# Gelu in one ScalarE activation in a fused attention and GEGLU kernel

## The chip, the cores and the metric

The kernel runs on one core of a Trainium2 chip. A core has five engines with a queue each: TensorE (PE, matrix products, with its weight loads shown apart as PEld), VectorE (DVE), ScalarE (ACT, activation functions), GpSimd (POOL) and SyncE (SP, which here only issues DMAs). The metric is the time of one execution on the device in microseconds; three runs of the kernel before were timed.

## The reference

A layer norm, then two branches of the same normalised rows, whose results are multiplied. `S` is 2048, `D` 576, `H` 32 heads of 18, `F` 4608, all in float32.

```python
xn = layernorm(x)
q, k, v = split(xn @ wqkv)                        # 32 heads of 18
s = concat(softmax(q @ k.T * 18 ** -0.5) @ v) @ wo
ff = (gelu(xn @ w_gate, approximate=True) * (xn @ w_up)) @ w_down
out = x + s * silu(ff)
```

The tanh form of Gelu is `0.5 * z * (1 + tanh(0.7978845608 * (z + 0.044715 * z ** 3)))`.

## The kernel before, in words

After a prologue (layer norm, transposes, the projections to q, k and v) the kernel is a row of 144 sections, `FF["n"]` counting them. A section computes the gate sums `pg` and the up sums `pu` of one block of 128 of the 4608 features for one block of 512 rows: 27 pairs of matmuls (`gate_up`, L422), one of a pair in the upper and one in the lower half of the array. Values are cut into a high and a low part, hence three products for each of nine chunks. Two sections (g = 0 and 1) make a step of the down projection (`down`, L538, tile `py`).

The first 11 sections run beside a part of the row maxima of attention. The next 128 each carry an eighth of a unit of attention between their pairs: eight times a pair of score matmuls (`score_pair`, L855, tile `pe`), whose exponentials ScalarE takes at once (L856, `pT`), and a pair of matmuls for a later unit's row maxima (`max_pair`, L809, tile `pm`), which VectorE reduces (L810). `spread` puts these 16 pairs between the 27. The last five of the 128 have no `pm`. Behind the pairs of a section stand the products with the values (`values`, L872, tile `acc`, 16 matmuls by the program and 32 in the trace's records), which use the section's own `pT`, and, after every section with g = 0, the 42 matmuls of `down`. Then come five last sections, whose activation is in `last_section`, with the output projection (L1026) beside them.

PE, ACT, DVE, POOL and SP take their instructions in the order of the program. PE's order is written by hand.

PSUM sets who waits for whom. `pg` and `pu` take two banks (tag `f`, two buffers). `pm`, `pe`, `py` and `acc` share three buffers of two banks each (`ring`, `RING` = 3): a `pe` or `pm` can only start when what stood in the buffer that it takes has been read, by an exponential on ACT or a reduction on DVE. Which of the three a tile takes is settled while the program is built.

Gelu is computed at the end of a section by `activate` (L427). In all but the last sections it runs with `early` true: ACT squares `pg` (L431), DVE makes `(pg² + 1/0.044715) * pg` (L432), ACT copies `pu` (L435), DVE multiplies that copy by `pg` (L436), ACT takes the tanh (L437), and DVE ends with `(tanh + 1) * t2` (L439). This h is twice Gelu times the up sums; the factor two is taken out again by the gates, with `scale=0.25` where silu is made of a tanh (L734, L1015, L1181) and a factor 0.25 in the last product (L1034, L1038).

Of the kernel before, what the change touches and what calls it, by code (L numbers as in the profile page):

```python
# [8 lines left out]
F32 = mybir.dt.float32  # L9
F32R = mybir.dt.float32r  # L10
AF = mybir.ActivationFunctionType
ALU = mybir.AluOpType
# [5 lines left out]
P = 128  # L18
# [38 lines left out]
ADD, SUB = ALU.add, ALU.subtract  # L57
COMBINED = (((6, ADD, 0), (5, ADD, 0)), ((6, SUB, 3), (5, ADD, 2)), ((6, SUB, 4), (5, SUB, 1)), ((4, ADD, 2), (1, SUB, 3)))
EPS = 1e-5
GC = 0.044715  # L60
GS = 0.7978845608028654
SCALE = DH ** -0.5


# [24 lines left out]
def kernel(ctx: ExitStack, tc: tile.TileContext, x, wqkv, wo, w_gate, w_up, w_down, out):  # L89
# [334 lines left out]

        return [lambda i=i: pair(i) for i in range(len(terms))], pg, pu

    def activate(pg, pu, g, early):  # L427

        h = ffn.tile([P, 3 + 3 * g, TH], F32, name=f"h{g}", bufs=2 - g)
        t1 = h[:, 0:2].rearrange("p a t -> p (a t)")  # L430
        nc.scalar.activation(t1, pg, AF.Square)  # L431
        nc.vector.scalar_tensor_tensor(t1, t1, 1.0 / GC, pg, op0=ALU.add, op1=ALU.mult)  # L432
        if early:
            t2 = ffn.tile([P, TB], F32, name="t2", bufs=1)
            nc.scalar.activation(t2, pu, AF.Copy)  # L435
            nc.vector.tensor_tensor(t2, t2, pg, op=ALU.mult)  # L436
        nc.scalar.activation(t1, t1, AF.Tanh, scale=GC * GS)  # L437
        if early:
            FF["last"] = lambda: nc.vector.scalar_tensor_tensor(t1, t1, 1.0, t2, op0=ALU.add, op1=ALU.mult)  # L439
        else:  # L440
            nc.vector.scalar_tensor_tensor(t1, t1, 1.0, pg, op0=ALU.add, op1=ALU.mult)
            nc.vector.tensor_tensor(t1, t1, pu, op=ALU.mult)
        return h


# [128 lines left out]
    def section(specials=(), tag="f", slots=False):  # L574

        n = FF["n"]
        FF["n"] += 1
        b, r = divmod(n // G, NR)
        g = n % G
        keep = tc.keep_in_program_order  # L580
        pairs, pg, pu = gate_up(tag)
        hooks, FF["hooks"] = FF["hooks"], {}

        def hook(i, what):
            hooks.setdefault(i, []).append(what)

        for i in range(n + 1, min(n + 3, NF)):
            if i not in FF["raw"]:
                FF["raw"][i] = load_gu(gu_part(i))
        nxt = FF["raw"].pop(n + 1, None)  # L590
        one = split_ap if n + 1 < ATT.start else split
        if nxt:
            for k in range(NG - 1):
                split_gu(nxt, k, one)
        if n == 0:
            load_rawd(0)
        if g == 0 and (b, r) in FORMED:
            raw = FF["rawd"]
            hook(12, lambda: sums_b(raw))
        new = n + 1 < NF and (n + 1) % (NR * G) == 0  # L600
        xd = []
        if new:
            for k in range(NG - 1):
                hook(9 * k + 9, lambda k=k: xd.append(load_xd(b + 1, k)))
        for p in spread(pairs, specials, 1 if slots else None, hooks):
            p()
        if nxt:
            split_gu(nxt, NG - 1, one)
        if n == 0:
            cut_plain_b(FF["rawd"])  # L610
        FF["w"] = nxt
        FF["act"] = activate(pg, pu, g, n < ATT.stop)
        if g > 0 or n not in ATT:
            FF.pop("last", lambda: None)()
        if new:
            xd.append(load_xd(b + 1, NG - 1))
            for t in hooks.get(len(pairs), ()):
                t()
            FF["xd"] = xd
# [5 lines left out]
    def finish():  # L625

        n = FF["n"] - 1
        b, r = divmod(n // G, NR)
        g, h, s = n % G, FF["act"], part(b, r)
        pool, vec, act = nc.gpsimd, nc.vector, nc.scalar  # L630
        keep = tc.keep_in_program_order
        FF.pop("last", lambda: None)()

        def hook(i, what):
            FF["hooks"].setdefault(i, []).append(what)

        def behind(what):
            what(keep if (n + 1) % (NR * G) == 0 else lambda i: i)

        late = (n + 2) % (NR * G) == 0 and n + 2 < NF  # L640
        if g == 1 and (b, r + 1) in NEXT:
            load_rawd(part(b, r + 1))
        if b == 0 and r < PLAIN:
            if g == 0 and r > 0:
                raw = FF["rawd"]
                hook(4, lambda: cut_plain_b(raw))
            cut_plain(g, h)
        elif (b, r) in FORMED:
            lead = n < ATT.start
            if g == 0:  # L650
                if lead:
                    hook(6, lambda: high_b(0))
                    hook(12, lambda: high_b(1))
                else:
                    high_b(0)
                    high_b(1)
                hook(9 if lead else 2, lambda: low_b(0))
                hook(16 if lead else 10, lambda: low_b(1))
                for k, i in enumerate((19, 24) if lead else (1, 3) if late else (13, 20)):
                    hook(i, lambda k=k: t_piece(s, k, True))  # L660
                sums_a(g, h, vec if lead else pool)
                hook(12, lambda: cut_a(0, h, pool, pool, keep))
            else:
                for k, i in enumerate((2, 9)):
                    hook(i, lambda k=k: t_piece(s, 2 + k, True))
                behind(lambda k: (sums_a(g, h, pool, k), cut_a(1, h, pool, pool, keep)))
        else:
            if g == 0:
                for k, i in enumerate((None, 5, 27, 27) if late else (None, 5, 13, 21)):
                    if i is None:  # L670
                        t_piece(s, k)
                    else:
                        hook(i, lambda k=k: t_piece(s, k))
            behind(lambda k: (sums_a(g, h, pool, k), cut_a(g, h, pool, pool, k)))
        if g == G - 1:
            FF["down"].append((b, r, n + 1))
# [54 lines left out]
    def gate(k, i):  # L731

        y, t = (t[:, i] for t in SC)
        nc.scalar.activation(t, y, AF.Tanh, scale=0.25)  # L734
        nc.gpsimd.tensor_tensor(t, t, y, op=ALU.mult)
        nc.gpsimd.tensor_tensor(y, y, t, op=ADD)

# [227 lines left out]
    with tc.tile_pool(name="epi", bufs=1, reuse_waits="tile") as epi:  # L965
# [45 lines left out]
        def gate(k):  # L1011
            if gated <= k < len(groups) and groups[k][0] < NB - 1:
                yy = YY[k % len(YY)]
                th = ffn.tile([P, D], F32, name="th", tag="h0", bufs=2)
                act.activation(th, yy, AF.Tanh, scale=0.25)  # L1015
                vec.scalar_tensor_tensor(yy, th, 1.0, yy, op0=ADD, op1=ALU.mult)

        def project(k):
# [11 lines left out]
        def multiply(k, po, c):  # L1030
            b, j = groups[k]
            t = YY[k % len(YY)].rearrange("p (c d) -> p c d", c=2)
            if b < NB - 1:
                vec.scalar_tensor_tensor(t[:, c], t[:, c], 0.25, po[:, c, 0:DC], op0=ALU.mult, op1=ALU.mult)  # L1034
            else:
                for i in range(2)[c]:
                    m = QUARTERS[2 * (j // 2) + i][2]
                    vec.scalar_tensor_tensor(t[:, i], FF["M"][:, m, j % 2], 0.25, po[:, i, 0:DC], op0=ALU.mult, op1=ALU.mult)  # L1038

        def finish_rows(k, c):  # L1040
            t, xx = (a[k % len(a)][:, DC * c.start:DC * c.stop] for a in (YY, XX))
# [26 lines left out]
        def last_section(tag):  # L1068

            n = FF["n"]  # L1070
            FF["n"] += 1
            g = n % G
            pairs, pg, pu = gate_up(tag)
            hooks, FF["hooks"] = FF["hooks"], {}
            nxt = FF["raw"].pop(n + 1, None)
            if nxt:
                split_gu(nxt, 0)
                split_gu(nxt, 1)
            for t in spread(pairs, (), 1, hooks):
                t()  # L1080
            if nxt:
                split_gu(nxt, 2)
            FF["w"] = nxt
            h = ffn.tile([P, 3 + 3 * g, TH], F32, name=f"h{g}", bufs=2 - g)
            t1 = h[:, 0:2].rearrange("p a t -> p (a t)")

            def gelu():
                act.activation(t1, pg, AF.Square)
                vec.scalar_tensor_tensor(t1, t1, 1.0 / GC, pg, op0=ADD, op1=ALU.mult)
                act.activation(t1, t1, AF.Tanh, scale=GC * GS)  # L1090
                vec.scalar_tensor_tensor(t1, t1, 1.0, pg, op0=ADD, op1=ALU.mult)
                vec.tensor_tensor(t1, t1, pu, op=ALU.mult)

            return h, gelu
# [83 lines left out]
        gate(n)  # L1178
        for i, c, m in QUARTERS:
            t = ffn.tile([P, 2, DC], F32, name="tg", tag=("h0", "h1")[c], bufs=2 - c)  # L1180
            act.activation(t, M[:, m], AF.Tanh, scale=0.25)  # L1181
            vec.scalar_tensor_tensor(M[:, m], t, 1.0, M[:, m], op0=ADD, op1=ALU.mult)
            for k in range({6: 1, 4: 2}.get(m, 0)):
                step()
# [30 lines left out]
```

## Time and profile before

| what | value |
|---|---|
| median of 3 runs | 2545.82 us (2545.0 to 2546.8) |
| span of the profiled execution | 2542.7 us |
| PE busy | 2534.6 us |
| DVE busy | 2092.2 us |
| POOL busy | 1620.2 us |
| ACT busy | 1452.9 us |
| three Gelu activations on ACT, all 139 of `activate` | 253.8 us |
| three Gelu operations on DVE, all 139 | 311.2 us |

The span runs from the first instruction to the last of the execution that the profiler recorded; of its own time the span is all that is known, 3.1 us below the median of the runs, and what lies around it is taken as those 3.1 us. Matmuls are pipelined: a row's duration reaches from a matmul's start to its modelled end, so two in a row overlap, and the distance of two starts tells what one costs. A row of the timeline may merge several instructions; its first columns are the start and the length in us from the start of the span, and in square brackets stands how long the engine had been idle and who ended that.

### The profile page before, as it was taken

The page shows a single profiled execution, that of the slowest core. Times are in us where ns is not written, and L with a number is a line of the kernel's source. Part 1 is how long each engine was busy: PE and PEld are TensorE (multiplying, and loading weights), DVE is VectorE, ACT ScalarE, POOL GpSimd, SP SyncE. Part 2 cuts the span into 40 slices and gives each one's busy share as a digit, 9 for nine tenths or more (in the row PEclk, how much of TensorE's full clock was granted, in tenths as well). Part 3 has the DMA queues.
Part 4 walks back from the last instruction along what each step waited for, and adds up shares of the span by engine and source line. Part 5 has one row for each costly group of instructions (what it writes and reads, how often), then busy time and mean ns, then how long its engine had stood idle before and what let it go on. Part 6 is the DMA issues. An engine that isn't in the chain of part 4 may idle for free.

```text
span 2542.7 us, 53140 instructions
## 1 busy us (share of the span) xinstructions
PE 2534.6 (100%) x20548; PEld 1837.5 (72%) x20548; DVE 2092.2 (82%) x2371; ACT 1452.9 (57%) x1753; POOL 1620.2 (64%) x1684
## 2 busy tenths in 40 slices
PE   9999999999999999999999999999999999999999
PEld 8888866667766676666667666776666676667689
DVE  5327888889888888888897898998898888888357
ACT  3223466666666665556666555655566665556621
POOL 3005688888888876666658565666667666666773
PEclk9999999999999999999999999999999999999999
DMA  8965465555685565667787777666668666665676
GB/s 259 312 207 136 117 176 158 163 162 164 168 252 147 165 173 146 167 163 166 172 221 187 172 167 169 172 169 164 155 158 236 167 172 173 164 168 154 190 188 236
DMA packets 416627, 455.04 MB, mean 179 GB/s; under 512 B 109428, under 2 KB 289396, under 8 KB 416376
## 3 DMA queue, kind: packets, MB, share of 16 engines
q1 hardware_dynamic: 416376, 451.64, 66.3%
q8 instruction: 164, 2.69, 0.5%
q14 instruction: 87, 0.71, 0.1%
HBM read 354.38 MB, written 97.13 MB: 178 GB/s over the span
## 4 chain that ended last, share of the span: by engine, by line
PE 97%; DVE 1%; POOL 1%; issue 0%; DMA 0%; ACT 0%; SPq 0%; DVEq 0%; POOLq 0%
PE pg L422 25%; PE acc L872 18%; PE py L538 15%; PE pm L809 9%; PE pe L855 9%; PE pu L422 9%; PE po L193 6%; PE po L1026 2%; PE pgu L422 2%; PE py L525 1%; PE pt L263 0%; POOL M L560 0%; DVE KA L756 0%; DMA xx<-in_A_x_dram 0%; DMA KA<-qk 0%
## 5 line engine op out<-in xcount | busy, mean ns | idle before, releaser
L856 ACT ACTIVATE pT<-pe 128x1024 f32<-128x1024 f32 x1024 | 1048.2, 1027 | 580.3 <-PE pe L855 544.5
L810 DVE TENSOR_REDUCE mx<-pm 128x2 f32<-128x1024 f32 x1024 | 1219.4, 1224 | 162.3 <-PE pm L809 145.7
L422 PE MATMUL pu<-xd,wh 64*128 64x512 f32 x2466 | 901.7, 396 | 0.0
L422 PE MATMUL pg<-xd,wh 64*128 64x512 f32 x2466 | 901.2, 396 | 0.0
L422 PEld LDWEIGHTS pg<-xd,wh 64*128 64x128 f32 x2466 | 454.5, 184 | 113.5 <-issue 55.4
L117 POOL TENSOR_SCALAR wh<-raw 128x384 fp32r<-128x384 f32 x402 | 211.8, 530 | 456.8 <-PE pu L422 275.3
L422 PE MATMUL pg<-xd,wl 64*128 64x512 f32 x1233 | 480.9, 390 | 0.3 <-POOL wl L124 0.3
L422 PE MATMUL pu<-xd,wl 64*128 64x512 f32 x1233 | 481.0, 390 | 0.0
L422 PEld LDWEIGHTS pu<-xd,wh 64*128 64x128 f32 x2466 | 454.3, 184 | 18.7
L872 PE MATMUL acc<-pT,VS 128*32 128x512 f32 x4096 | 466.0, 595 | 0.0
L119 POOL TENSOR_TENSOR wl<-raw,wh 128x384 fp32r<-128x384 f32 x402 | 422.4, 1054 | 26.4
L809 PE MATMUL pm<-KA,QT 64*128 64x512 f32 x2048 | 410.9, 393 | 0.4 <-ACT pT L856 0.3
L855 PE MATMUL pe<-QT,KA 64*128 64x512 f32 x2048 | 409.0, 391 | 0.3 <-DVE mx L810 0.3
L538 PE MATMUL py<-T,ah 128*128 128x288 f32 x1876 | 380.6, 298 | 0.0
L545 DVE TENSOR_TENSOR M<-py,M 128x576 f32<-128x576 f32 x448 | 338.8, 758 | 31.4 <-PE py L538 18.2
L538 PEld LDWEIGHTS py<-T,ah 128*128 128x128 f32 x1876 | 298.3, 188 | 54.0 <-issue 54.0
L451 POOL TENSOR_TENSOR al<-h,ah 128x512 fp32r<-128x512 f32 (+1 forms) x143 | 295.3, 2065 | 51.6 <-ACT ah L448 37.9
L872 PEld LDWEIGHTS acc<-pT,VS 128*32 128x32 f32 x4096 | 120.2, 109 | 276.6 <-issue 229.6
L538 PE MATMUL py<-T,al 128*128 128x288 f32 x938 | 275.6, 294 | 0.0
L855 PEld LDWEIGHTS pe<-QT,KA 64*128 64x128 f32 x2048 | 191.9, 184 | 110.8 <-DVE mx L810 25.5
L422 PEld LDWEIGHTS pg<-xd,wl 64*128 64x128 f32 x1233 | 227.3, 184 | 33.8 <-POOL wl L124 0.7
L422 PEld LDWEIGHTS pu<-xd,wl 64*128 64x128 f32 x1233 | 227.5, 185 | 10.4
(167 smaller groups left out, 2943.5 us busy)
## 6 DMA issues: line engine op xcount, KB each, us to landing
T<-ts SPq DMA_DIRECT2D x98, 576.0 KB
KA<-qk SPq DMA_DIRECT2D x768, 72.0 KB
T<-ts SPq DMA_DIRECT2D x98, 432.0 KB
raw<-in_B_w_gate_dram SPq DMA_DIRECT2D x144, 288.0 KB
raw<-in_B_w_up_dram SPq DMA_DIRECT2D x144, 256.0 KB
ts<-T SPq DMA_DIRECT2D x36, 576.0 KB
VS<-vs SPq DMA_DIRECT2D x128, 152.0 KB
qk<-t SPq DMA_DIRECT2D x72, 256.0 KB
```

The lines of the kernel that those rows point to most:

```text
L117: first = nc.gpsimd.tensor_scalar(hi, raw, 1.0, 1.0, op0=ALU.mult, op1=ALU.mult)
L119: keep(nc.gpsimd.tensor_tensor(lo, raw, f(hi), op=ALU.subtract))
L193: nc.tensor.matmul(o, st, m, start=(i == 0), stop=(i == len(terms) - 1))
L422: nc.tensor.matmul(o, w[1 + wp][k][rr, c, :], xd[k][xp][rr, c, :], start=(i == 0), stop=(i == len(terms) - 1))
L451: low = two.tensor_tensor(lo, raw, f(hi), op=ALU.subtract)
L538: nc.tensor.matmul(py[:, t, 0:DC], h[:, i, tt], T[:, w, k], start=n == 0, stop=n == 2)
L545: nc.vector.tensor_tensor(M[:, m], py[:, :, 0:DC], M[:, m], op=ALU.add)
L809: nc.tensor.matmul(pm[:, a], QS[u, r][rr, t * P:(t + 1) * P], KS[(u * NA + c) % KB][r][rr, :], start=True, stop=True)
L810: nc.vector.tensor_reduce(MX[u][:, 2 * r:2 * r + 2, t, c], pm, axis=AX.X, op=ALU.max)
L855: nc.tensor.matmul(pe[:, a], KS[(u * NA + c) % KB][r][rr, t * P:(t + 1) * P], QS[u, r][rr, :], start=True, stop=True)
L856: nc.scalar.activation(PT[u, kt][:, 2 * r:2 * r + 2, :], pe, AF.Exp, scale=SCALE)
L872: nc.tensor.matmul(ACC[u][32 * a:32 * a + 32, :], VS[(u * NA + c) % VB][:, v:v + 32], pt[:, a, :], start=first, stop=last, skip_group_chec ...
```

## The change

Gelu becomes one activation with ScalarE's function for the tanh form, and one VectorE product with `pu`, in `activate` and in `last_section`. The result is no longer doubled, so the gates go from 0.25 to 0.5. The `early` case with its copy and its delayed last product (`FF["last"]`) is gone.

```diff
-    def activate(pg, pu, g, early):
+    def activate(pg, pu, g):
         h = ffn.tile([P, 3 + 3 * g, TH], F32, name=f"h{g}", bufs=2 - g)
         t1 = h[:, 0:2].rearrange("p a t -> p (a t)")
-        nc.scalar.activation(t1, pg, AF.Square)
-        nc.vector.scalar_tensor_tensor(t1, t1, 1.0 / GC, pg, op0=ALU.add, op1=ALU.mult)
-        if early:
-            t2 = ffn.tile([P, TB], F32, name="t2", bufs=1)
-            nc.scalar.activation(t2, pu, AF.Copy)
-            nc.vector.tensor_tensor(t2, t2, pg, op=ALU.mult)
-        nc.scalar.activation(t1, t1, AF.Tanh, scale=GC * GS)
-        if early:
-            FF["last"] = lambda: nc.vector.scalar_tensor_tensor(t1, t1, 1.0, t2, op0=ALU.add, op1=ALU.mult)
-        else:
-            nc.vector.scalar_tensor_tensor(t1, t1, 1.0, pg, op0=ALU.add, op1=ALU.mult)
-            nc.vector.tensor_tensor(t1, t1, pu, op=ALU.mult)
+        nc.scalar.activation(t1, pg, AF.Gelu_apprx_tanh)
+        nc.vector.tensor_tensor(t1, t1, pu, op=ALU.mult)
         return h
...
-        FF["act"] = activate(pg, pu, g, n < ATT.stop)
-        if g > 0 or n not in ATT:
-            FF.pop("last", lambda: None)()
+        FF["act"] = activate(pg, pu, g)
...
-        nc.scalar.activation(t, y, AF.Tanh, scale=0.25)
+        nc.scalar.activation(t, y, AF.Tanh, scale=0.5)
...
             def gelu():
-                act.activation(t1, pg, AF.Square)
-                vec.scalar_tensor_tensor(t1, t1, 1.0 / GC, pg, op0=ADD, op1=ALU.mult)
-                act.activation(t1, t1, AF.Tanh, scale=GC * GS)
-                vec.scalar_tensor_tensor(t1, t1, 1.0, pg, op0=ADD, op1=ALU.mult)
+                act.activation(t1, pg, AF.Gelu_apprx_tanh)
                 vec.tensor_tensor(t1, t1, pu, op=ALU.mult)
```

In the built program this also puts table loads on ACT's queue, ACT_TABLE_LOAD, one ahead of each activation whose function is not in the table that is loaded: 259 of them, where the program before has 2. Of the new ones 129 stand ahead of a Gelu and 128 ahead of the first exponential of a section. ACT's rows at the end of one section of attention and the start of the next, before (`pT` is an exponential, `h` and `t` belong to Gelu, `accs` takes the sums of `acc`; the brackets name the engines whose semaphores an instruction waits for):

```order
L856 ACTIVATE pT<-pe 128x1024 [waits PE_49]
L431 ACTIVATE h_7956<-pg 128x512 [waits PE_49]
L435 ACTIVATE t_7959<-pu 128x512 [waits DVE_49,PE_49]
L437 ACTIVATE h_7956<-h_7956 128x512 [waits DVE_49]
L876 ACTIVATE accs<-acc 128x512 [waits DMAHW3_49,PE_49]
L856 ACTIVATE pT<-pe 128x1024 [waits PE_49,Activation_49]
```

The same place in the changed program (L841 is the exponential now, L429 the Gelu, L861 the copy of `acc`):

```order
L841 ACTIVATE pT<-pe 128x1024 [waits PE_49]
L429 ACT_TABLE_LOAD [waits DVE_49]
L429 ACTIVATE h_7801<-pg 128x512 [waits PE_49]
L861 ACTIVATE accs<-acc 128x512 [waits DMAHW3_49,DVE_49,PE_49]
L841 ACT_TABLE_LOAD [waits PE_49]
L841 ACTIVATE pT<-pe 128x1024 [waits Activation_49]
```

Of three activations one is left, and two loads have come; the exponential's wait for PE has gone over to the load ahead of it. Of the 128 loads at L841, 127 wait for PE so.

PE's matmuls stand in the same order as before, but the buffers of the ring are handed out in another turn at the start of a section. PE's rows from the second `pm` of a section to its third `pe`, before:

```order
L809 MATMUL pm<-KA,QT_1951 128x512 [waits Activation_49]
L809 MATMUL pm<-KA,QT_1951 128x512
L422 MATMUL pg<-xd_0_8750,wh 128x512
L422 MATMUL pu<-xd_0_8750,wh 128x512
L855 MATMUL pe<-QT_1953,KA 128x512 [waits DVE_49]
L855 MATMUL pe<-QT_1953,KA 128x512
```

The same rows in the changed program (L794 is `pm`, L840 `pe`, L420 the gate and up pairs):

```order
L794 MATMUL pm<-KA,QT_1951 128x512 [waits DVE_49]
L794 MATMUL pm<-KA,QT_1951 128x512
L420 MATMUL pg<-xd_0_8575,wh 128x512
L420 MATMUL pu<-xd_0_8575,wh 128x512
L840 MATMUL pe<-QT_1953,KA 128x512 [waits Activation_49]
L840 MATMUL pe<-QT_1953,KA 128x512
```

In 122 of the sections the second `pm` takes the buffer of the first `pm`, so it waits for the first reduction, and the third `pe` takes that of the first `pe`, so it waits for the first exponential; before it was the other way about. From the third `pm` on the turn is as it was: each `pm` waits for the exponential of the slot before its own. SP's queue is the same row for row.

More of the change, by code (lines that the diff above doesn't have):

```diff
@@ L59 @@
 EPS = 1e-5
-GC = 0.044715
-GS = 0.7978845608028654
 SCALE = DH ** -0.5
@@ L631, in finish @@
         keep = tc.keep_in_program_order
-        FF.pop("last", lambda: None)()
         def hook(i, what):
@@ L1014, in gate @@
                 th = ffn.tile([P, D], F32, name="th", tag="h0", bufs=2)
-                act.activation(th, yy, AF.Tanh, scale=0.25)
+                act.activation(th, yy, AF.Tanh, scale=0.5)
                 vec.scalar_tensor_tensor(yy, th, 1.0, yy, op0=ADD, op1=ALU.mult)
@@ L1033, in multiply @@
             if b < NB - 1:
-                vec.scalar_tensor_tensor(t[:, c], t[:, c], 0.25, po[:, c, 0:DC], op0=ALU.mult, op1=ALU.mult)
+                vec.scalar_tensor_tensor(t[:, c], t[:, c], 0.5, po[:, c, 0:DC], op0=ALU.mult, op1=ALU.mult)
             else:
@@ L1037, in multiply @@
                     m = QUARTERS[2 * (j // 2) + i][2]
-                    vec.scalar_tensor_tensor(t[:, i], FF["M"][:, m, j % 2], 0.25, po[:, i, 0:DC], op0=ALU.mult, op1=ALU.mult)
+                    vec.scalar_tensor_tensor(t[:, i], FF["M"][:, m, j % 2], 0.5, po[:, i, 0:DC], op0=ALU.mult, op1=ALU.mult)
         def finish_rows(k, c):
@@ L1180 @@
             t = ffn.tile([P, 2, DC], F32, name="tg", tag=("h0", "h1")[c], bufs=2 - c)
-            act.activation(t, M[:, m], AF.Tanh, scale=0.25)
+            act.activation(t, M[:, m], AF.Tanh, scale=0.5)
             vec.scalar_tensor_tensor(M[:, m], t, 1.0, M[:, m], op0=ADD, op1=ALU.mult)
```

## The prediction

> **What bounds the kernel now.** The page comes first: busy time, granted clock, and the chain that ended last.
>
> ```profile
> span 2542.7 us, 53140 instructions
> PE 2534.6 (100%) x20548; PEld 1837.5 (72%) x20548; DVE 2092.2 (82%) x2371; ACT 1452.9 (57%) x1753; POOL 1620.2 (64%) x1684
> ...
> PEclk9999999999999999999999999999999999999999
> ...
> PE 97%; DVE 1%; POOL 1%; issue 0%; DMA 0%; ACT 0%; SPq 0%; DVEq 0%; POOLq 0%
> ```
>
> TensorE has work for the whole span, at its full clock, and the chain of waits is 97% PE. So work taken from ACT or DVE saves no time by itself; the change can only matter where PE waits for one of them. Whether it does is read from one section of attention. The timeline of PE, then of ACT and of DVE, at the end of a section and in the next (1222.45 is its first pair), and one weight load:
>
> ```profile
> 1218.88 3.64 PE L872 MATMUL acc<-pT,VS 128*32 128x512 f32 x32
> 1222.45 0.49 PE L422 MATMUL pg<-xd,wh 64*128 64x512 f32 x1
> 1222.79 0.39 PE L855 MATMUL pe<-QT,KA 64*128 64x512 f32 x2
> 1223.24 0.40 PE L809 MATMUL pm<-KA,QT 64*128 64x512 f32 x2
> 1223.94 0.39 PE L855 MATMUL pe<-QT,KA 64*128 64x512 f32 x2
> 1224.63 0.40 PE L809 MATMUL pm<-KA,QT 64*128 64x512 f32 x2
> 1224.87 0.40 PE L422 MATMUL pg<-xd,wh 64*128 64x512 f32 x1
> 1225.10 0.39 PE L855 MATMUL pe<-QT,KA 64*128 64x512 f32 x2
> 1225.79 0.40 PE L809 MATMUL pm<-KA,QT 64*128 64x512 f32 x2
> 1226.94 0.39 PE L809 MATMUL pm<-KA,QT 64*128 64x512 f32 x2
> ...
> 1216.96 2.15 ACT L856 ACTIVATE pT<-pe 128x1024 f32<-128x1024 f32 x2 [0.42 <-PE pe L855]
> 1219.04 0.60 ACT L431 ACTIVATE h<-pg 128x512 f32<-128x512 f32 x1
> 1223.28 2.12 ACT L856 ACTIVATE pT<-pe 128x1024 f32<-128x1024 f32 x2 [2.04 <-PE pe L855]
> ...
> 1220.49 0.68 DVE L436 TENSOR_TENSOR t<-t,pg 128x512 f32<-128x512 f32 x1
> 1221.28 0.69 DVE L439 SCALAR_TENSOR_TENSOR h<-h,t 128x512 f32<-128x512 f32 x1
> 1223.71 2.59 DVE L810 TENSOR_REDUCE mx<-pm 128x2 f32<-128x1024 f32 x2 [0.27 <-PE pm L809]
> ...
> 1224.99 0.19 PEld L855 LDWEIGHTS pe<-QT,KA 64*128 64x128 f32 x2 [0.16 <-DVE mx L810]
> ```
>
> Pairs follow each other every 0.23 us without a hole. Gelu lies wholly under the value products: its last reader of a bank that the next section needs, L436, ends at 1221.17, and the next pair starts at 1222.45. But the ring is tight: the third `pm`, at 1225.79, needs the second exponential, which ends at 1225.40.
>
> **The change part by part.** The groups of instructions by shape, first of ACT, then of DVE, give the durations:
>
> ```profile
> L856 ACT ACTIVATE pT<-pe 128x1024 f32<-128x1024 f32 x1024 | 1048.2, 1027 | 580.3 <-PE pe L855 544.5 <-PE pu L422 2.3
> L437 ACT ACTIVATE h<-h 128x512 f32<-128x512 f32 x139 | 87.8, 631 | 67.9 <-DVE h L432 67.9
> L435 ACT ACTIVATE t<-pu 128x512 f32<-128x512 f32 x134 | 80.4, 600 | 0.0
> L431 ACT ACTIVATE h<-pg 128x512 f32<-128x512 f32 x134 | 79.6, 594 | 10.5 <-PE pu L422 8.7 <-PE pg L422 1.6 <-issue 0.2
> L810 DVE TENSOR_REDUCE mx<-pm 128x2 f32<-128x1024 f32 x1024 | 1219.4, 1224 | 162.3 <-PE pm L809 145.7
> L439 DVE SCALAR_TENSOR_TENSOR h<-h,t 128x512 f32<-128x512 f32 x139 | 122.5, 881 | 14.3 <-ACT h L437 0.5
> L436 DVE TENSOR_TENSOR t<-t,pg 128x512 f32<-128x512 f32 x134 | 91.1, 680 | 0.0
> L432 DVE SCALAR_TENSOR_TENSOR h<-h,pg 128x512 f32<-128x512 f32 x134 | 90.8, 678 | 47.7 <-ACT h L431 47.7
> L1092 DVE TENSOR_TENSOR h<-h,pu 128x512 f32<-128x512 f32 x3 | 2.1, 686 | 0.2
> ```
>
> Removed: 139 times 631, 600 and 594 ns on ACT (253.7 us) and 881, 680 and 678 ns on DVE (311.2 us). Added: 139 activations that I price at 594 ns, the square's row, which reads and writes the same shapes (82.6 us), and 139 products at 686 ns (95.4 us). DVE ends some 216 us lighter. In attention this is worth nothing on the path, since the value products cover it. The stretches with the first eleven sections and with the last five and the output (start and end, length, busy time of PE, PEld, DVE, ACT and POOL, granted clock):
>
> ```profile
> 160.00:280.00 120.00, 119.73 (x888) 103.09 (x888) 79.82 (x99) 42.10 (x79) 44.18 (x36) 1.00 0.51 138
> 2430.00:2543.00 113.00, 107.67 (x844) 101.12 (x844) 75.70 (x104) 24.14 (x39) 57.00 (x50) 0.99 0.75 233
> ```
>
> PE is busy for all but 0.3 and 5.3 us; a lighter Gelu can give back between nothing and 5.6 us, and I take nothing, because most of it lies in the end, behind the last Gelu. The gates at 0.5 cost what they cost at 0.25.
>
> The table loads cost. The built program has 257 more. The trace has one between two activations, in the prologue:
>
> ```profile
> 152.97 0.41 ACT L324 ACTIVATE vn<-po 128x288 f32<-128x288 f32 x1 [1.46 <-PE po L193]
> 153.41 1.28 ACT L356 ACT_TABLE_LOAD   x1
> 154.70 0.20 ACT L356 ACTIVATE eps<-eps 128x1 f32<-128x1 f32 x1
> ```
>
> It starts 0.03 us after its predecessor's end, takes 1.28 us, and its successor follows 0.01 us behind. So 1.30 us a switch, and 257 × 1.28 = 329 us more on ACT, which would come to 1453 − 254 + 83 + 329 = 1611 us.
>
> Not every switch is on the path. *Ahead of a Gelu:* the last exponential of a section ends at 1219.11 (1216.96 + 2.15). Load to 1220.42, Gelu to 1221.02, product to 1221.74, and 0.16 us from a release to the matmul (below): 1221.9. The next pair is due at 1222.45; 0.55 us are left, more where `down` stands between. h is ready at 1221.74 where it was at 1221.97, so POOL's sums behind it aren't late. Cost nothing; the value products hide it.
>
> *Ahead of a section's first exponential:* the load itself waits for the scores, so it can't use the 2.04 us in which ACT idles before them. Behind it queue all eight exponentials, and PE's ring waits for those. With the load from 1223.28 the first exponential runs from 1224.58 to 1225.61, the second, close behind (0.99 us apart, by the row of eight below), ends at 1226.60 (each 1.03). A release reaches PE as at 1224.94, where the first reduction ends (1223.71 + 1.23), its weight load follows at 1224.99 and its matmul at 1225.10: 0.16 us. Then the new turn of the buffers:
>
> - Second `pm`, now behind the first reduction: 1224.94 + 0.16 = 1225.10 for 1224.63, 0.47 us late. This holds with no load at all.
> - Third `pe`, 0.47 us behind it, now behind the first exponential: 1225.61 + 0.16 = 1225.77 for 1225.10, 0.67 late.
> - Third `pm`, 0.69 us behind, behind the second exponential: 1226.60 + 0.16 = 1226.76 for 1225.79, 0.97 late.
> - Fourth `pm`: due at 1226.94 + 0.97 = 1227.91. The third exponential, 0.99 behind the second, ends at 1227.59, released by 1227.75. The stall ends here, since a slot of PE takes 1.15 us (1225.79 to 1226.94) and an exponential 0.99.
>
> So a section loses 0.97 us, and not 1.30, because the ring had some 0.3 us in hand. The rest of the section moves with it. The five sections without `pm` are bound by ACT:
>
> ```profile
> 2354.12 7.94 ACT L856 ACTIVATE pT<-pe 128x1024 f32<-128x1024 f32 x8 [2.04 <-PE pe L855]
> ```
>
> Eight exponentials in 7.94 us without a pause: there the whole 1.30 us counts. In the first of the 128 the load waits for nothing; I take it as hidden.
>
> Sum: 122 × 0.97 + 5 × 1.30 = 118.3 + 6.5 = 124.8 us on the span of 2542.7, which gives 2667.5; with the 3.1 us between this span and the median of the runs (2545.82), 2671 us, 4.9% slower. SP's and POOL's orders stay, and every DMA has the more time.
>
> Bounds of the loss in a section: 0.47 if the load hides, 1.30 if nothing is in hand. I stay at 0.97, since each of its terms has a row.
>
> **The rivals.** *A switch costs twice the load.* If ACT had to empty besides, for as long again, each first exponential would be 1.28 us later, and Gelu at the 64 section ends without `down` would miss its 0.55 us by 0.73: 128 × (0.97 + 1.28) + 64 × 0.73 = 335 us, 2881 us. The rows speak against it: 0.03 us before the load and 0.01 behind. They are one case, though, behind a short activation of 0.41 us. The Trainium skill's page "ScalarE: Activation LUTs", section "What ACT_TABLE_LOAD costs", states this rule: a load of about 1283 ns and a drain of about 1380 ns, some 2.66 us a switch. The trace agrees with the load (1.28 us) and shows no such drain. By the page's figure the sum, an estimate, would be 128 × 2.35 + 64 × 0.83 = 354 us, 2900 us.
>
> *The load hides, the turn stays.* ACT is idle for 2.04 us ahead of the first exponential, and Gelu ends at 1221.0, so a load at once would be over at 1222.3, before 1223.28. Then only the 0.47 us of the second `pm` is left: 122 × 0.47 = 57 us, 2603 us. Against it: 127 of the loads stand behind the wait for the scores.
>
> *Faster, because DVE is lighter.* At the end of a section the value products wait for a reduction:
>
> ```profile
> 1232.33 0.39 PE L422 MATMUL pg<-xd,wh 64*128 64x512 f32 x1
> 1232.65 0.16 PEld L872 LDWEIGHTS acc<-pT,VS 128*32 128x32 f32 x8 [0.37 <-DVE mx L810]
> ```
>
> The pair at 1232.33 needs 0.23 us, so PE loses 0.09 us, in 128 sections 11 us. If DVE's reductions ran ahead by that much and the loads hid, the time would be 2534 us. It is decided by the load's start: by 1222.0 it is hidden, at 1223.28 it is not. And DVE's reductions are paced by `pm`, not by Gelu. *The same* would need loads that cost nothing and the old turn.
>
> **How the numbers follow.** The forecast has 0.79, the double price 0.08, the hidden load 0.07, faster 0.03, the same 0.03. A difference under 0.2% (5 us) can't be told from none here. Faster 0.03, same 0.03, slower 0.94. The forecast's own range goes from 0.8 us a section, the 0.97 less PE's 0.09 at the end and as much again at a release (2648 us), to 1.30 in all 128 with 0.4 us lost at the 64 ends without `down` (2546 + 166 + 26 = 2738). The range reaches down to the hidden load, 2603, and up to 2740, and leaves out the double price, the same and faster.
>
> **What would show it.** In the changed profile: 259 loads of 1.28 us; the first exponential of a section 1.3 us later against its scores; the weight loads of `pm` and `pe` waiting for `pT`, about 1 us a section; the 10.2 us from a section's first pair to its value products (1222.45 to 1232.65) becoming 11.2; ACT near 1611 us and DVE near 1876; PE's busy time short of the span by roughly the loss. I am wrong if exponentials trail a load by more than 0.1 us, if the first pair of a section waits for Gelu's product, or if PE waits for nothing new.

## The result, and the profile after

The change is slower: 2647.07 us (median of 4 runs, 2646.63 to 2648.11) against 2545.89 us before, a ratio of 1.0398 with a 95% interval of 1.0383 to 1.0413. That is 101 us more; the forecast was 125 us more. The profiled execution's span grew from 2542.7 to 2645.2 us, by 102.5 us.

The page of the changed kernel, its spans, its chain of waits, and the two groups of table loads on ACT:

```profile
span 2645.2 us, 52933 instructions
PE 2613.4 (99%) x20548; PEld 1812.7 (69%) x20548; DVE 1906.3 (72%) x2083; ACT 1607.5 (61%) x1727; POOL 1595.6 (60%) x1684
...
PEclk9999999999999999999999999999999999999999
...
PE 93%; DVE 6%; issue 1%; ACT 0%; DMA 0%; SPq 0%; DVEq 0%; ACTq 0%
```

```profile
L429 ACT ACT_TABLE_LOAD x129 | 165.5, 1283 | 2.6 <-issue 0.4
L841 ACT ACT_TABLE_LOAD x128 | 164.2, 1283 | 421.2 <-PE pe L840 417.9
```

257 more loads of 1283 ns are on ACT, and DVE has 186 us less to do, yet it is DVE that now has 6% in the chain. One section tells why. The timeline of the changed kernel for a section that starts at 1266.48, PE, ACT, DVE, then the weight loads that wait:

```profile
1262.91 3.64 PE L857 MATMUL acc<-pT,VS 128*32 128x512 f32 x32
1266.82 0.39 PE L840 MATMUL pe<-QT,KA 64*128 64x512 f32 x2
1267.28 0.39 PE L794 MATMUL pm<-KA,QT 64*128 64x512 f32 x2
1267.97 0.39 PE L840 MATMUL pe<-QT,KA 64*128 64x512 f32 x2
1269.02 0.50 PE L794 MATMUL pm<-KA,QT 64*128 64x512 f32 x2 [0.20 <-DVE mx L795]
1269.67 0.50 PE L840 MATMUL pe<-QT,KA 64*128 64x512 f32 x2
1270.58 0.50 PE L794 MATMUL pm<-KA,QT 64*128 64x512 f32 x2
1277.49 2.78 PE L857 MATMUL acc<-pT,VS 128*32 128x512 f32 x24
...
1263.16 1.28 ACT L429 ACT_TABLE_LOAD   x1
1264.46 0.60 ACT L429 ACTIVATE h<-pg 128x512 f32<-128x512 f32 x1
1267.30 1.28 ACT L841 ACT_TABLE_LOAD   x1 [2.24 <-PE pe L840]
1268.59 2.86 ACT L841 ACTIVATE pT<-pe 128x1024 f32<-128x1024 f32 x3
...
1265.09 0.69 DVE L430 TENSOR_TENSOR h<-h,pu 128x512 f32<-128x512 f32 x1 [1.07 <-ACT h L429]
1267.74 1.23 DVE L795 TENSOR_REDUCE mx<-pm 128x2 f32<-128x1024 f32 x1 [0.27 <-PE pm L794]
...
1266.48 0.18 PEld L420 LDWEIGHTS pg<-xd,wh 64*128 64x128 f32 x1 [0.84 <-issue]
1269.02 0.19 PEld L794 LDWEIGHTS pm<-KA,QT 64*128 64x128 f32 x2 [0.63 <-DVE mx L795]
1269.66 0.19 PEld L840 LDWEIGHTS pe<-QT,KA 64*128 64x128 f32 x2 [0.34 <-ACT pT L841]
1270.58 0.19 PEld L794 LDWEIGHTS pm<-KA,QT 64*128 64x128 f32 x2 [0.38 <-ACT pT L841]
```

ACT idles 2.24 us for the scores and only then loads the table. The first exponential starts 1.77 us behind its matmul (1266.82 to 1268.59) where it was 0.49 us. PE then waits three times, in the order that the prediction gave: the second `pm` for the first reduction (released at 1268.97, started at 1269.02), the third `pe` for the first exponential, the third `pm` for the second. After that nothing more is late. From the first pair to the value products it is 11.01 us (1266.48 to 1277.49) where it was 10.20 (1222.45 to 1232.65). The chain of waits runs through the first reduction of each section and shows nothing of the load (ACT has 0%): it takes the two stalls behind it for longer matmuls. Behind the last section nothing changed: from the last value product's start to the end of the span it is 119.1 us in both profiles (2542.7 − 2423.6, 2645.2 − 2526.1).

### The profile page after: what moved, and what is told of

It is laid out like the page before. It is cut to its first block, busy times and chain, and to the rows that moved or that the text cites. A ratio compares the mean times of both kernels' runs of the same rounds, so it can differ in the third digit from the quotient of the medians.

```text
span 2645.2 us, 52933 instructions
## 1 busy us (share of the span) xinstructions
PE 2613.4 (99%) x20548; PEld 1812.7 (69%) x20548; DVE 1906.3 (72%) x2083; ACT 1607.5 (61%) x1727; POOL 1595.6 (60%) x1684
## 4 chain that ended last, share of the span: by engine, by line
PE 93%; DVE 6%; issue 1%; ACT 0%; DMA 0%; SPq 0%; DVEq 0%; ACTq 0%
PE pg L420 27%; PE acc L857 17%; PE py L526 15%; PE pm L794 11%; PE pe L840 9%; PE po L191 7%; DVE mx L795 6%; PE po L1011 2%; PE pgu L420 2%; PE pu L420 2%; PE py L513 1%; PE pt L261 0%; DMA xx<-in_A_x_dram 0%; ACT pT L841 0%; DVE ol L994 0%
## 5 line engine op out<-in xcount | busy, mean ns | idle before, releaser
L841 ACT ACTIVATE pT<-pe 128x1024 f32<-128x1024 f32 x1024 | 1019.0, 1027 | 146.0 <-PE pe L840 124.6
L420 PE MATMUL pu<-xd,wh 64*128 64x512 f32 x2466 | 901.4, 396 | 0.0
L420 PE MATMUL pg<-xd,wh 64*128 64x512 f32 x2466 | 899.8, 395 | 0.0
L420 PEld LDWEIGHTS pg<-xd,wh 64*128 64x128 f32 x2466 | 455.3, 185 | 120.6 <-issue 53.7
L115 POOL TENSOR_SCALAR wh<-raw 128x384 fp32r<-128x384 f32 x402 | 206.1, 515 | 511.1 <-PE pu L420 351.4
L420 PE MATMUL pg<-xd,wl 64*128 64x512 f32 x1233 | 482.1, 391 | 0.0
L420 PE MATMUL pu<-xd,wl 64*128 64x512 f32 x1233 | 481.9, 391 | 0.0
L420 PEld LDWEIGHTS pu<-xd,wh 64*128 64x128 f32 x2466 | 456.3, 185 | 10.4 <-DVE h L430 0.4
L794 PE MATMUL pm<-KA,QT 64*128 64x512 f32 x2048 | 431.8, 418 | 24.5 <-DVE mx L795 23.6
L117 POOL TENSOR_TENSOR wl<-raw,wh 128x384 fp32r<-128x384 f32 x402 | 405.8, 1013 | 26.3
L841 ACT ACT_TABLE_LOAD x128 | 164.2, 1283 | 421.2 <-PE pe L840 417.9
L840 PE MATMUL pe<-QT,KA 64*128 64x512 f32 x2048 | 418.8, 403 | 0.0
L794 PEld LDWEIGHTS pm<-KA,QT 64*128 64x128 f32 x2048 | 193.2, 184 | 161.0 <-DVE mx L795 77.2
L840 PEld LDWEIGHTS pe<-QT,KA 64*128 64x128 f32 x2048 | 193.3, 184 | 122.4 <-ACT pT L841 42.6
```

The costliest lines, as they stand in the source:

```text
L115: first = nc.gpsimd.tensor_scalar(hi, raw, 1.0, 1.0, op0=ALU.mult, op1=ALU.mult)
L117: keep(nc.gpsimd.tensor_tensor(lo, raw, f(hi), op=ALU.subtract))
L420: nc.tensor.matmul(o, w[1 + wp][k][rr, c, :], xd[k][xp][rr, c, :], start=(i == 0), stop=(i == len(terms) - 1))
L794: nc.tensor.matmul(pm[:, a], QS[u, r][rr, t * P:(t + 1) * P], KS[(u * NA + c) % KB][r][rr, :], start=True, stop=True)
L840: nc.tensor.matmul(pe[:, a], KS[(u * NA + c) % KB][r][rr, t * P:(t + 1) * P], QS[u, r][rr, :], start=True, stop=True)
L841: nc.scalar.activation(PT[u, kt][:, 2 * r:2 * r + 2, :], pe, AF.Exp, scale=SCALE)
```

## The experiments

The theory is the prediction's: the table load behind the scores costs the time, through the ring of three buffers, whose new turn has a part of its own. Its rivals: the arithmetic (Gelu's function or the lighter DVE) is what changes the time; or the turn alone does.

**The exponentials' table loaded early.** One tiny exponential on a spare column (it lies in the tile split_rows), right behind each Gelu of attention; ACT's queue order is given by `behind`. Dots stand for lines of an edit that are left out here, in this run those that make the column.

```diff
...
-        nc.scalar.activation(t1, pg, AF.Gelu_apprx_tanh)
+        one = nc.scalar.activation(t1, pg, AF.Gelu_apprx_tanh)
+        if FF["n"] - 1 in ATT:
+            behind(nc.scalar.activation(tiny, tiny, AF.Exp, scale=-1.0), one)
         nc.vector.tensor_tensor(t1, t1, pu, op=ALU.mult)
```

> The change with one tiny exponential (128x1) right behind each Gelu of the attention sections, so that the table of the exponentials is loaded while ACT idles and not behind the scores; the program then also has the old turn of the ring buffers again. If the load behind the scores is the loss: 2545 us (2538 to 2552), still 259 to 261 loads of 1.28 us, no weight load of a section waiting for pT beyond the few of before. If Gelu's activation or the lighter DVE work itself were the loss: 2647 us, as the change.

2544.37 us (11 runs) against 2546.32, ratio 0.9992 (0.9983 to 1.0000). The whole loss is gone while all the loads are still there: two at each section's end, with the exponential where it was in the kernel before, 0.50 us behind its scores. The weight loads of `pm` wait for `pT` 12 times in all, 14 times before.

```profile
1217.58 1.28 ACT L431 ACT_TABLE_LOAD   x1
1218.87 0.60 ACT L431 ACTIVATE h<-pg 128x512 f32<-128x512 f32 x1
1219.49 1.28 ACT L433 ACT_TABLE_LOAD   x1
1220.78 0.20 ACT L433 ACTIVATE split_rows<-split_rows 128x1 f32<-128x1 f32 x1
1221.76 2.12 ACT L845 ACTIVATE pT<-pe 128x1024 f32<-128x1024 f32 x2 [0.77 <-PE pe L844]
...
1221.26 0.39 PE L844 MATMUL pe<-QT,KA 64*128 64x512 f32 x2
```

So it is where a load stands that costs, not that it is there. The ring has its old turn in this run too; the two runs on the turn, below, tell the one from the other. This kernel and the one before differ by 2 us, less than the 0.2% (5 us) that the prediction takes as the least that can be told from none.

**The old Gelu with the loads.** The six operations of before, and a tiny Gelu behind each tanh.

```diff
...
-        nc.scalar.activation(t1, t1, AF.Tanh, scale=GC * GS)
+        one = nc.scalar.activation(t1, t1, AF.Tanh, scale=GC * GS)
+        if early:
+            behind(nc.scalar.activation(tiny, tiny, AF.Gelu_apprx_tanh), one)
```

> The kernel before, its Gelu in six operations kept, with one tiny Gelu (128x1) behind each tanh, so that 257 loads come in: one ahead of the tiny Gelu and one ahead of each section's first exponential; the ring takes the new turn by itself. If loads and turn are the loss: 2647 us (2635 to 2660), about 0.8 us a section. If the new arithmetic is: 2546 us.

2649.28 us (4 runs), ratio 1.0406 (1.0391 to 1.0420): the change's loss without the change's arithmetic.

**The light arithmetic without loads.** A plain tanh takes Gelu's place.

```diff
-        nc.scalar.activation(t1, pg, AF.Gelu_apprx_tanh)
+        nc.scalar.activation(t1, pg, AF.Tanh)
...
-                act.activation(t1, pg, AF.Gelu_apprx_tanh)
+                act.activation(t1, pg, AF.Tanh)
```

> The change with a plain tanh in the place of the Gelu function (the result is another one), so that the arithmetic is light and no load comes in; the turn of the ring is the old one. If removed ACT and DVE work is worth nothing: 2545 us (2541 to 2548), the 0.9 us that the first eleven sections gave included. If a lighter DVE helps PE at the section ends (0.09 us in 128): 2534 us.

2543.90 us (11 runs), ratio 0.9990 (0.9981 to 0.9999). Two activations and two DVE operations fewer in each section are worth 2.4 us (0.3 to 4.8 by the interval), less than the 5 us named above. The 2534 us of a lighter DVE did not come.

**Loads with the old turn of the buffers.** Three tags of one buffer each in the place of one tag of three, taken in the order in which they were given out last (a gate and up tile that lies in the ring is left out while it is held).

```diff
-    def ring(name):
+    TURN, HELD = [0, 1, 2], []
+    def ring(name, skip=0):
-        return ps.tile([P, 2, TB], F32, name=name, tag="ring", bufs=RING)
+        i = [t for t in TURN if t not in HELD][skip]
+        TURN.remove(i)
+        TURN.append(i)
+        if name == "pgu":
+            HELD.append(i)
+        return ps.tile([P, 2, TB], F32, name=name, tag=f"ring{i}", bufs=1)
...
```

> The change with the three ring buffers named by hand in the old turn: the second pm of a section waits for the first exponential again. By the working of the prediction the second pm is then late by the whole load less what the ring had in hand: first exponential's end to the matmul 1.13 us late by that reckoning, 1.0 with the rows of the changed profile, so 122 x 1.0 to 1.13: 2670 to 2690 us. If the turn makes no difference: 2647 us. If the turn is the whole loss: 2546 us.

2678.62 us (4 runs), ratio 1.0520 (1.0504 to 1.0536): 132 us, or 1.08 us in each of 122 sections, as the working of the prediction has it for that turn. PE now makes one stall of the three, at the second `pm` behind the first exponential:

```profile
1280.84 0.40 PE L848 MATMUL pe<-QT,KA 64*128 64x512 f32 x2
1283.69 0.51 PE L802 MATMUL pm<-KA,QT 64*128 64x512 f32 x2 [0.83 <-ACT pT L849]
...
1282.62 1.95 ACT L849 ACTIVATE pT<-pe 128x1024 f32<-128x1024 f32 x2
```

**The new turn without loads.** The kernel before with the same ring, and `skip=1` for the second `pm` of 122 sections.

```diff
...
-            pm = ring("pm")
+            pm = ring("pm", 1 if swapped and place == 1 else 0)
```

> The kernel before, no loads added, with the ring buffers named by hand so that 122 sections take the new turn: the second pm waits for the first reduction, the third pe for the first exponential. If the prediction's 0.47 us stands: 122 x 0.47 = 57 us, 2603 us. If the load is the whole loss and the turn nothing: 2546 us. If the turn is the whole loss: 2647 us.

2602.41 us (4 runs) against 2546.05, ratio 1.0219 (1.0205 to 1.0233): 56 us, 0.46 us in each of 122 sections, at the place expected:

```profile
1252.37 0.51 PE L820 MATMUL pm<-KA,QT 64*128 64x512 f32 x2 [0.20 <-DVE mx L821]
```

The span of its profiled execution is 58.8 us longer than before; 55.7 us of that lie in the 122 sections, the rest ahead of them.

With this the four cases are complete: no load and old turn 2546 us, no load and new turn 2602, load and old turn 2679, load and new turn 2647. The new turn costs 56 us by itself, but where the load is, it saves 31 us (a loss of 101 for one of 132), because the second `pm` waits for a reduction that is early instead of an exponential that is late.

**A longer Gelu.** The early exponential's kernel with each Gelu of attention done three times over.

```diff
         one = nc.scalar.activation(t1, pg, AF.Gelu_apprx_tanh)
+        if FF["n"] - 1 in ATT:
+            for k in range(2):
+                one = nc.scalar.activation(t1, pg, AF.Gelu_apprx_tanh)
```

> The early exponential's kernel with each Gelu of attention done three times over, so that the product that frees pu comes about 1.3 us later. In the changed profile 0.65 us are left between a release by the product and the next section's first pair. If that is the cover of Gelu's load: the 64 section ends without a down projection lose 0.65 us each, 42 us, 2587 us (2570 to 2600). If the cover is larger or pu isn't waited for: 2545 us.

2590.89 us (4 runs) against 2546.05, ratio 1.0173 (1.0159 to 1.0187), 45 us or 0.70 us at each of 64 section ends. The second matmul of the first pair waits for the product:

```profile
PEld pu L422 <- DVE h L437: 31.0, 64, 0.8
```

```profile
1237.91 0.60 ACT L431 ACTIVATE h<-pg 128x512 f32<-128x512 f32 x1
1238.54 1.23 ACT L434 ACTIVATE h<-pg 128x512 f32<-128x512 f32 x2
1239.85 0.69 DVE L437 TENSOR_TENSOR h<-h,pu 128x512 f32<-128x512 f32 x1 [2.39 <-ACT h L434]
...
1239.93 0.18 PEld L422 LDWEIGHTS pg<-xd,wh 64*128 64x128 f32 x1 [0.84 <-issue]
1240.60 0.18 PEld L422 LDWEIGHTS pu<-xd,wh 64*128 64x128 f32 x1 [0.48 <-DVE h L437]
```

So the cover of Gelu's own load is real and not wide: the two Gelus more end 1.26 us behind the first (1238.51 to 1239.77) and cost 0.67 us here (1239.93 to 1240.60), so 0.59 us of them were covered.

**The slots one place earlier.** The early exponential's kernel with the first score pair ahead of the first gate and up pair.

```diff
-        for p in spread(pairs, specials, 1 if slots else None, hooks):
+        for p in spread(pairs, specials, 0 if slots else None, hooks):
```

> The early exponential's kernel with the 16 score and maximum pairs of a section one place earlier among the 27 pairs (first slot ahead of pair 0). The last reductions then end 0.23 us earlier against the value products, which wait 0.09 us for one in each section. If nothing else comes late: 2534 us. If the first slot now runs into a wait of its own (buffers of the ring at the section's start): 2545 us or more.

2544.83 us (11 runs), ratio 0.9994 (0.9985 to 1.0003): nothing. The wait for a reduction at the value products is gone from its row, but the gap is not:

```profile
1218.40 0.16 PEld L861 LDWEIGHTS acc<-pT,VS 128*32 128x32 f32 x8 [0.36 <-issue]
...
1218.06 0.39 PE L422 MATMUL pg<-xd,wh 64*128 64x512 f32 x1
```

The pair at 1218.06 needs 0.23 us and the products start at 1218.40, 0.11 us late where it was 0.09, and no engine is waited for. The five sections without `pm` have no reduction to wait for, and there too the weight load idles for 0.36 us (at 2480.95 in the changed profile). What makes that gap, between a pair's matmul and the first value product, is open.

## Why the prediction was right, and where its size was off

The bound by PE, and nothing for the work removed: right, by the plain tanh (2543.9 us). Gelu's load under the value products: right in the sections with `pm`. In the changed profile the product ends at 1265.78 (1265.09 + 0.69) and the next section starts at 1266.48; with 0.05 us for the release that leaves 0.65 us. The forecast was 0.55, with 0.16 us for the release, and the longer Gelu gave 0.59.

The stall at a section's start: the right three waits, in the right order, and the right first term (0.47 forecast, 0.46 measured alone). Its end was mis-sized: 0.97 us forecast, 0.81 in the section shown and 0.84 in the mean of the 122. From the first pair of the first of them to the first pair behind the last they took 2028.98 us before (324.31 to 2353.29) and 2131.73 after (323.33 to 2455.06), 102.75 us more. The first exponential is as forecast, 2.11 us behind the section's start (1268.59 − 1266.48) for 2.13. The term that failed is the distance between exponentials, 0.99 us. It came from the row of eight in 7.94 us, which the prediction read as eight without a pause on a bound ACT. The same eight after the change:

```profile
2457.17 7.44 ACT L841 ACTIVATE pT<-pe 128x1024 f32<-128x1024 f32 x8
```

With the scores all waiting, seven distances take 7.44 − 1.03 us, 0.92 each. So the row before was paced by PE's scores, although it shows no idle time: the first and the eighth score pair of that section start at 2353.62 and 2360.55, 0.99 us from one to the next as well. In the section above, three exponentials take 2.86 us: the second ends at 1270.53, 4.05 us from the start for 4.15 forecast. That is 0.10 of the 0.16 us. Some 0.04 more come back later in the section. Before, the fifth `pe` waited for a reduction, and the pair behind it came 0.27 us later in place of 0.23:

```profile
1227.57 0.19 PEld L855 LDWEIGHTS pe<-QT,KA 64*128 64x128 f32 x2 [0.21 <-DVE mx L810]
```

In the changed section that wait is gone. The 0.02 us that are left are of the size of the rounding of the rows.

The same misreading made the term for the five sections without `pm`: 1.30 us each, since ACT was taken as their bound. It isn't. In the section that starts at 2455.06 after the change, the eight exponentials end 9.55 us behind the first pair (at 2464.61), where it was 8.77 (2362.06 − 2353.29). Yet the value products start 8.25 us behind the first pair, for 8.28 before: nothing is lost inside the section. What is lost is lost at its end. The later exponentials push Gelu and its product back, and where no `down` stands between, the next section's first pair waits for the product:

```profile
2484.18 0.69 DVE L430 TENSOR_TENSOR h<-h,pu 128x512 f32<-128x512 f32 x1 [10.65 <-ACT h L429]
...
2484.52 0.18 PEld L420 LDWEIGHTS pg<-xd,wh 64*128 64x128 f32 x1 [0.84 <-issue]
2484.92 0.18 PEld L420 LDWEIGHTS pu<-xd,wh 64*128 64x128 f32 x1 [0.22 <-DVE h L430]
```

The profile has two such waits, at the starts of the third and the fifth of these sections, and these two are longer. From first pair to first pair the first four take 17.60, 11.86, 18.00 and 11.87 us, for 17.62, 11.85, 17.62 and 11.85 before; the fifth takes 0.35 us more to its last value product. That is 0.75 us in all for 6.5 forecast. The prediction had named a first pair that waits for Gelu's product as a sign of being wrong, and at these two ends it was wrong about the cover, which it had worked out for a section with `pm` alone.

The stretches of the two profiles give the sum: 102.75 us in the 122 sections (122 × 0.84 for 122 × 0.97 forecast) and 0.75 us in the last five, less 1.0 us that what lies ahead of the 122 sections gave (323.33 for 324.31, forecast nothing), make the 102.5 us of the span. One sign that the prediction named didn't come: PE's busy time is 31.8 us short of the span (8.1 before), not short by the loss, since a matmul's row is longer than the distance of two starts (0.39 to 0.50 us for 0.23), and a short stall leaves little of a gap.

The rivals. Twice the load: wrong. All 129 loads ahead of a Gelu together had 2.6 us of idle time ahead of them, and in the section shown Gelu and the first exponential follow their loads by 0.02 us and 0.01. The drain of about 1380 ns that the Trainium skill's page "ScalarE: Activation LUTs", section "What ACT_TABLE_LOAD costs", adds to a switch doesn't show in this trace; the load of about 1283 ns does. The hidden load with the turn left over: its price, 2603 us, is what the new turn without loads measured (2602). Faster by a lighter DVE: its price rested on the 0.09 us ahead of the value products being a wait for DVE, by the label of a weight load's idle time; earlier slots removed the label and left the gap, so there was nothing to win.

ACT's busy time came to 1607.5 us for 1611 forecast. DVE's came to 1906.3 for 1876: the lengths of all its rows together fell by 218 us (2172 to 1954), near the 216 forecast, but rows that follow each other closely overlap, so the time in which it was busy fell by 186 us only.

## What to carry to other kernels

One activation need not be cheaper than several if its table is another one: count the loads that the built program has, and see for each what its activation waits for. A load that takes over the wait of the activation behind it can't use the idle time of that wait and runs behind it; a tiny activation of the coming function, put where the engine idles, moves it away (here, with the old turn of the buffers, that took away the whole loss). And see whether the distance in a row of merged instructions is the engine's own or that of what feeds it, before it is used as the engine's pace.

## What the runs showed that was not expected

Exponentials of 1.03 us start 0.92 us apart when all their scores are ready (eight in 7.44 us); when scores come one by one the same row shows no idle time up to 0.99 us apart (eight in 7.94 us), and 1.09 us for a pair that is fed (2.12 us for two). The turn in which three buffers are given out, settled while the program is built, was worth 56 us of loss without the loads and 31 us of gain with them, without one instruction of PE in another place.
